# Attention and a maxout FFN on one core: batch 0 reordered, and loads issued behind the crossbar transpose's shift

## The chip, the cores and the metric

The kernel runs on one core of one Trainium2 chip. Time is device microseconds of that core, the median of repeated runs. The profile is one execution, recorded by the hardware profiler; instants in it are counted from its first instruction.

## The reference

Softmax attention with an extra exp(−m) in the denominator, then a feed-forward network whose hidden layer is the maximum of three products:

```python
scores = scale * np.matmul(q, k.transpose(0, 1, 3, 2))      # q, k, v: (8, 12, 448, 64)
m = np.max(scores, axis=-1, keepdims=True)
e = np.exp(scores - m)
attn = e / (np.sum(e, axis=-1, keepdims=True) + np.exp(-m) + 1e-09)
attn_out = np.matmul(attn, v)
x = attn_out.transpose(0, 2, 1, 3).reshape(B * S, H * D)    # 3584 x 768
h = np.maximum(np.maximum(x @ w1, x @ w2), x @ w3)          # 768 x 768 each
out = h @ w_out
```

Inputs and output are float32; the kernel computes in float16 with float32 sums.

## The kernel before

**Units of work.** The eight batches have twelve heads each. Four heads form a group, so a batch has three groups and there are 24 of them, numbered 0 to 23. For a group, `load_qk` (L91) and `load_v` (L108) bring q, k and v to SBUF and cast them to float16; POOL issues these loads. q and k must be transposed. Groups below `PE_QK` (6) are transposed by TensorE with an identity, `transpose_pe` (L172), and copied out of PSUM by DVE or ACT. Later groups go through the DMA crossbar, `transpose_dma` (L207): one DMA for QT and one for KT, issued by SP. QT then needs blocks copied to the other half of the partitions, `shift_q` (L216), four copies on POOL.

**Attention.** `scores` (L260) multiplies KT blocks with QT into PSUM tiles `stp` of the pool `ps_s` (three buffers), and ACT takes the exponential into `e`. `av_tail` (L304) and `av_main` (L323) multiply `e` with v, which `prep_v` (L354) has arranged in `vx` and `vt`; a column of constants beside v gives the sum of the exponentials. DVE adds the one, inverts and scales, into `xn`. `x_transpose_pe` (L367, TensorE and DVE) or `x_transpose_dma` (L382, a crossbar DMA from SP) puts `xn` into `xT`.

**FFN.** `up_piece` (L392) makes one slice of the hidden layer for one of the three weights: six matmuls for each 128 features in a tile `p_i` of the pool `ps_b` (two buffers), and DVE copies it or takes the maximum into `hT`. `out_piece` (L418) makes half of 128 output rows: six matmuls into `op_ps`, a scaling copy on DVE into `o_sb` (three buffers), and after the second half two stores of 64 rows from SP.

**Order.** The order on each engine is written out by hand. FFN pieces stand in a list; `fill` (L467) takes pieces from it while a credit in matmul columns lasts, so that FFN matmuls lie between attention matmuls.

- Batch 0 runs in six parts: its three groups with the even tokens ("E"), then with the odd ones ("O"). Part n computes scores of its group, then `av` of the part before, and at its end the x transpose of the part before. After the fourth part (n = 3), `add_up` puts nine FFN pieces for the even tokens in the list.
- From group 3 on, iteration i has three visits: scores of a third of group i in each, `av` of group i−1 in the first two, `prep_v(i)` and the x transpose of group i−1 in the second, and FFN pieces at the end of each. `adds` names the visits at which a further batch's FFN pieces enter the list; `share` spreads what is in the list over the visits until the next such visit.
- Iteration i begins with `transpose_dma(i + 2)` (SP), then the loads of v for group i+2 and of q and k for group i+3 (POOL), then the visits, and it ends with `shift_q(i + 2)` (POOL). QT and KT have three buffers, so the transpose of group i+2 waits for the scores of group i−1, and for the loads of group i+2. Each engine and each queue works in order: what stands behind a waiting instruction on SP or POOL waits too.

The lines that set this order in an iteration:

```python
        if i + 2 < NI and i + 2 >= PE_QK:
            transpose_dma(i + 2)
        ...
        elif i + 2 < NI:
            load_v(i + 2)
            if i + 3 < NI:
                load_qk(i + 3)
        for vi, units in enumerate(visits):
        ...
        if i + 2 < NI and i + 2 >= PE_QK:
            shift_q(i + 2, nc.gpsimd)
```

The functions in full:

Of the kernel before, what the change touches and what calls it, by code (L numbers as in the profile page):

```python
# [21 lines left out]
def kernel(  # L22
# [29 lines left out]
    scale = 1.0 / math.sqrt(D)  # L52


    PE_QK = 6
    NEB = 2
    NV = 3

# [32 lines left out]
    def load_qk(i, names="kq", prs=(0, NP)):  # L91
        b, g = groups[i]
        tiles = raw.setdefault(i, {})
        for nm in names:
            if nm not in tiles:
                t = ld_pool.tile([P, NP * T + 2, D], MMDT, tag="ld_" + nm, name="ld_" + nm)
                if nm == "q" and i < PE_QK:
                    nc.vector.memset(t[:, 0 : NP * T + 2 : NP * T + 1, :], 0.0)
                tiles[nm] = t
            src = {"q": q, "k": k}[nm][b].rearrange("h s d -> (h s) d")  # L100
            src = src.rearrange("(g r x t) d -> g x r (t d)", g=NG, r=NP, x=P)[g]
            p0, p1 = prs
            nc.gpsimd.dma_start(  # L103
                out=tiles[nm][:, 1 : NP * T + 1].rearrange("x (r t) d -> x r (t d)", r=NP)[:, p0:p1],
                in_=src[:, p0:p1],
            )
# [24 lines left out]
    nc.vector.memset(wz, 0.0)  # L131
    load_qk(0, "q")
    load_qk(0, "k", (0, 1))
    ident16 = cpool.tile([128, 128], MMDT, name="ident16")
    make_identity(nc, ident16)
    load_qk(0, "k", (1, 2))
    load_qk(1)
    load_v(0)
    load_qk(2)
# [32 lines left out]
    def transpose_pe(i, pr, pool, k_eng, q_engs):  # L172

        if pool is ps_s:
            both = ps_s.tile([128, 2, 1024], MMDT, tag="s", name="trT")
            tps = [both[:, 0], both[:, 1]]
        else:
            tps = [ps_b.tile([128, 1024], MMDT, tag="b", name="trT") for _ in range(2)]
        kr, qr = raw[i]["k"], raw[i]["q"]
        def tr(n, j, src, t):  # L180
            nc.tensor.transpose(  # L181
                out=tps[n][:, ts(j, 128)],
                in_=src[:, t + 1 : t + 3, :].rearrange("x t d -> x (t d)"),
                identity=ident16,
            )

        kj = (0, 1, 2) if pr == 0 else (3, 4, 5, 6)
        qt = (-1, 1, 3, 5, 0, 2, 4, 6) if pr == 0 else (8, 10, 12, 7, 9, 11, 13)
        for j, b in enumerate(kj):
            tr(0, j, kr, 2 * b)  # L190
        for j, t in enumerate(qt):
            tr(1, j, qr, t)
        if i not in KT:
            KT[i] = att_pool.tile([P, T * 128], MMDT, tag="KT", name="KT")
            QT[i] = att_pool.tile([P, (NB + 1) * 128], MMDT, tag="QT", name="QT")
        evac(
            k_eng,
            KT[i][:, kj[0] * 128 : (kj[-1] + 1) * 128],
            tps[0][:, 0 : len(kj) * 128],
        )  # L200
        q0 = pr * 1024
        n = -(-len(qt) // len(q_engs))
        for e, eng in enumerate(q_engs):
            a, b = e * n * 128, min((e + 1) * n, len(qt)) * 128
            evac(eng, QT[i][:, q0 + a : q0 + b], tps[1][:, a:b])
# [209 lines left out]
    NW = DM // NH  # L415
    order = (0, 2, 4, 6, 1, 3, 5)

    def out_piece(bp, t, nh):  # L418
        if nh == 0:
            outs[0] = out_pool.tile([128, DM], FP32, tag="o_sb", name="o_sb")  # L420
        o_sb = outs[0]
        op_ps = ps_b.tile([128, 512], FP32, tag="b", name="op_ps")
        for fc in range(NFC):
            nc.tensor.matmul(  # L424
                out=op_ps[:, 0:NW],
                lhsT=hT[bp][:, fc, ts(t, 128)],
                rhs=wout_sb[:, fc, ts(nh, NW)],
                start=(fc == 0),
                stop=(fc == NFC - 1),
            )  # L430
        nc.vector.tensor_scalar(  # L431
            out=o_sb[:, ts(nh, NW)],
            in0=op_ps[:, 0:NW],
            scalar1=1.0 / LAMBDA,
            scalar2=None,
            op0=ALU.mult,
        )
        if nh == NH - 1:
            for half in range(2):
                n = 2 * t + half  # L440
                b = 2 * bp + n // T
                rows = out[b * S : (b + 1) * S].rearrange("(p t) m -> t p m", t=T)
                nc.sync.dma_start(out=rows[order[n % T]], in_=o_sb[half * HP : half * HP + HP])


    UP = NDC * (S + 6)
# [3 lines left out]
    def add_up(b, q0, qn, order):  # L450
        w = 1 if qn == S else 2
        for i, f0 in order:
            fcs = tuple(range(f0, f0 + w))
            pieces.append((up_piece, (b, fcs, i, q0, qn), NDC * w * (qn + 6)))
# [12 lines left out]
    def fill(cols):  # L467
        credit[0] += cols
        while pieces and credit[0] > 0:
            f, a, w = pieces.pop(0)  # L470
            f(*a)
            credit[0] -= w
        if not pieces:
            credit[0] = min(credit[0], 0.0)
# [5 lines left out]
    DV, AC = nc.vector, nc.scalar  # L480
    warm(10)
    transpose_pe(0, 0, ps_s, DV, (AC, DV))
    transpose_pe(0, 1, ps_b, DV, (DV,))
    load_weight(0)
    prep_v(1, nc.gpsimd)
# [3 lines left out]

    parts = [(part, g) for part in "EO" for g in range(NG)]  # L490
    PW = {"E": (0, 1), "O": (2, 3), "EO": (0, 1, 2, 3)}
    UPE = 9 * 2 * NDC * (NE + 6) / 10

    def av(i, ej, pr, part):
        av_tail(i, ej, pr, PW[part])
        av_main(i, ej, pr, PW[part])

    for n, (part, g) in enumerate(parts):
        ej = n % NEB
        pp, pg = parts[n - 1] if n > 0 else (None, None)  # L500
        step = UPE if n > 3 else 0
        scores(g, ej, (0, 1), part)
        scores(g, ej, (2, 3), part)
        if n > 0:
            av(pg, 1 - ej, 0, pp)
        fill(step)
        if part == "E" and 0 < g < NG - 1:
            transpose_pe(g + 1, 0, ps_b, AC, (DV,))
        fill(step)
        scores(g, ej, (4, 5), part)  # L510
        scores(g, ej, (6,), part)
        if n > 0:
            av(pg, 1 - ej, 1, pp)
        if n == 0:
            transpose_pe(1, 0, ps_b, DV, (DV,))
        fill(step)
        if part == "E" and g < NG - 1:
            transpose_pe(g + 1, 1, ps_b, DV, (DV,))
        if n == 5:
            transpose_pe(3, 1, ps_s, DV, (DV,))  # L520
        fill(step)
        if n == 0:
            prep_v(0, DV)
        if n > 0:
            x_transpose_pe(pg, pp)
        if n == 1:
            load_weight(2)
        if n == 2:
            load_v(3)
            load_qk(4)  # L530
            load_weight(3)
        if n == 3:
            add_up(0, 0, NE, [(i, f) for i in range(3) for f in (0, 2, 4)])
        if n == 4:
            load_v(4)
            load_qk(5)
            transpose_pe(3, 0, ps_s, DV, (DV,))


    visits = ((0, 1), (2, 3), (4, 5, 6))  # L540
    adds = {3 * (3 * b + 4) + 1: b for b in range(1, B - 1)}

    def share(n):

        nxt = min([a for a in adds if a > n], default=3 * NI + 2)
        return left() / (nxt - n)

    for i in range(3, NI):
        ej, pj = (i + 1) % NEB, i % NEB
        first = i == 3  # L550
        if i + 2 < NI and i + 2 >= PE_QK:
            transpose_dma(i + 2)
        if first:
            load_v(5)
            load_qk(6)
        elif i + 2 < NI:
            load_v(i + 2)
            if i + 3 < NI:
                load_qk(i + 3)
        for vi, units in enumerate(visits):  # L560
            n = 3 * i + vi
            scores(i, ej, units)
            if vi < 2:
                av(i - 1, pj, vi, "O" if first else "EO")
            if vi == 1:
                prep_v(i, nc.vector if i < PE_QK else nc.gpsimd)
                if not first:
                    x_transpose_dma(i - 1)
            if n in adds:
                add_batch(adds[n])  # L570
            per = UPE if first and vi < 2 else share(n)
            if vi == 2 and first:
                fill(per / 2)
                x_transpose_pe(i - 1, "O")
                add_up(0, NE, NO, [(w, f) for w in range(3) for f in (0, 2, 4)])
                add_out(0)
                per = share(n)
            if vi > 0 and i + 1 < PE_QK:
                fill(per / 2)
                transpose_pe(i + 1, vi - 1, ps_s, DV, (DV,))  # L580
                fill(per / 2)
            else:
                fill(per)
        if i + 2 < NI and i + 2 >= PE_QK:
            shift_q(i + 2, nc.gpsimd)

    av(NI - 1, NI % NEB, 0, "EO")
    av(NI - 1, NI % NEB, 1, "EO")
# [34 lines left out]
```

## Time and profile before

| what | us |
|---|---|
| median of 13 runs (lowest, highest) | 348.16 (344.98, 356.18) |
| the profiled execution's own time | 347.0 |
| its span in the profile | 345.1 |
| TensorE (PE) busy | 329.1 |
| VectorE (DVE) busy | 191.7 |
| ScalarE (ACT) busy | 146.2 |
| GpSimd (POOL) busy | 139.4 |
| TensorE's last matmul ends | 340.0 |

The profiled execution's time is 1.9 us longer than its span, which runs from the first to the last instruction, and 1.2 us under the median of the runs. Busy times overlap, so they don't add up to the span. A busy PE means that a matmul is under way, not that the array is full; the mean clock granted to it was 0.994 of full speed. Instructions that only issue a DMA are not busy time on SP and ACT; on POOL they are.

### The profile page before, as it was taken

What the parts mean: (1) busy time and instruction counts of PE and PEld (TensorE: products, weight loads), DVE (VectorE), ACT (ScalarE), POOL (GpSimd) and SP (SyncE); (2) the same over time, 40 slices, a digit from 0 to 9 for tenths busy, and PEclk for the clock granted to TensorE, in tenths of its full rate; (3) what the DMA queues carried; (4) which work ended last, traced back from release to release, by engine and by line L of the source; (5) the groups of instructions that cost most, each with busy time, mean ns of one, the idle gap of its engine ahead of it and who ended that gap; (6) DMA issues with size and microseconds to landing.
All of it is one profiled execution on the core that took longest, in us unless ns stands there. A gap on an engine that the chain in (4) does not pass through costs nothing.

```text
span 345.1 us, 9731 instructions
## 1 busy us (share of the span) xinstructions
PE 329.1 (95%) x4150; PEld 198.8 (58%) x4150; DVE 191.7 (56%) x418; ACT 146.2 (42%) x174; POOL 139.4 (40%) x247
## 2 busy tenths in 40 slices
PE   7869989899999999999999999999999999999994
PEld 3547768765555555556555555556555555565552
DVE  2654576765555555555556556556556555565552
ACT  2863354676444435443443443444443443400000
POOL 8684540566094607633857065173535000000000
PEclk9998999999999999999999999999999999999999
DMA  7999999999999999999996999979951450124006
GB/s 95 192 207 209 205 201 143 146 118 198 145 180 148 164 141 220 155 94 157 226 171 106 178 180 136 146 87 233 166 95 21 123 123 3 31 62 108 2 16 167
DMA packets 89499, 47.42 MB, mean 137 GB/s; under 512 B 58224, under 2 KB 85872, under 8 KB 89456
## 3 DMA queue, kind: packets, MB, share of 16 engines
q0 software_dynamic: 29392, 22.03, 47.5%
q1 hardware_dynamic: 60064, 24.78, 43.6%
q8 instruction: 32, 0.52, 0.7%
q14 instruction: 11, 0.09, 0.1%
HBM read 44.04 MB, written 11.01 MB: 160 GB/s over the span
## 4 chain that ended last, share of the span: by engine, by line
PE 88%; DMA 4%; DVE 3%; issue 2%; ACT 2%; POOL 1%; ACTq 0%; POOLq 0%
PE p_i L401 46%; PE op_ps L424 16%; PE avp L331 11%; PE stp L274 11%; DMA ld_q<-in_q_dram 3%; PE avp L314 2%; ACT e L294 2%; PE trT L181 2%; DMA ld_k<-in_k_dram 1%; DVE xn L347 0%; DVE QT L170 0%; PE xtp L374 0%; POOL ld_k L103 0%; DVE hT L412 0%; DVE vt L360 0%
## 5 line engine op out<-in xcount | busy, mean ns | idle before, releaser
L294 ACT ACTIVATE e<-stp 128x896 f16<-128x896 f32 (+4 forms) x171 | 143.8, 903 | 147.8 <-PE stp L274 147.8
L401 PE MATMUL p_i<-xT,w 128*128 128x448 f16 (+2 forms) x972 | 174.4, 333 | 0.1
L401 PEld LDWEIGHTS <-w 128*128 128x128 f16 x972 | 90.4, 98 | 68.3 <-issue 5.0
L412 DVE TENSOR_TENSOR hT<-hT,p_i 128x448 f16<-128x448 f16 (+2 forms) x96 | 59.5, 621 | 42.3 <-PE p_i L401 42.0
L219 POOL COPY QT<-QT 64x384 f16<-64x384 f16 (+1 forms) x72 | 40.1, 556 | 104.1 <-DMA QT<-ld_q 73.9
L424 PE MATMUL op_ps<-w,hT 128*128 128x384 f16 x336 | 58.3, 326 | 0.4 <-DVE hT L412 0.4
L274 PE MATMUL stp<-QT,KT 64*64 64x448 f16 (+2 forms) x756 | 47.9, 339 | 3.9 <-ACT e L294 3.5
L331 PE MATMUL avp<-vx,e 128*128 128x65 f16 x1152 | 45.6, 194 | 0.0
L424 PEld LDWEIGHTS <-hT 128*128 128x128 f16 x336 | 31.6, 98 | 23.6 <-issue 2.6
L431 DVE TENSOR_SCALAR o_sb<-op_ps 128x384 f32<-128x384 f32 x56 | 31.1, 556 | 24.8 <-PE op_ps L424 24.8
L410 DVE CAST hT<-p_i 128x448 f16<-128x448 f32 (+2 forms) x48 | 30.0, 624 | 24.2 <-PE p_i L401 24.1
L331 PEld LDWEIGHTS <-e 128*128 128x128 f16 x1152 | 39.0, 98 | 2.3
L347 DVE TENSOR_TENSOR xn<-avp,rb 128x512 f16<-128x512 f32 (+1 forms) x54 | 34.1, 632 | 1.9
L341 DVE TENSOR_SCALAR rb<-avp 128x8 f32<-128x8 f32 (+1 forms) x54 | 8.9, 165 | 43.5 <-PE avp L331 43.5
L274 PEld LDWEIGHTS <-KT 64*64 64x64 f16 x756 | 15.8, 105 | 28.3 <-issue 25.1
L314 PEld LDWEIGHTS <-e 64*64 64x64 f16 x768 | 14.9, 108 | 8.3 <-issue 1.7
L103 POOL DMA_DIRECT2D ld_q<-in_q_dram x24 | 17.9, 744 | 4.2 <-DMA w<-in_moe_w_dram 1.2
L103 POOL DMA_DIRECT2D ld_k<-in_k_dram x25 | 17.9, 715 | 3.1 <-PE p_i L401 1.5
L357 POOL COPY vx<-ld_v 128x768 f16<-128x768 f16 x20 | 16.4, 818 | 5.5 <-issue 2.9
L314 PE MATMUL avp<-vt,e 64*64 64x65 f16 x768 | 15.7, 193 | 1.1 <-ACT e L294 0.8
L113 POOL DMA_DIRECT2D ld_v<-in_v_dram x24 | 15.1, 628 | 3.7 <-DMA ld_k<-in_k_dram 1.7
L116 POOL DMA_DIRECT2D ld_v<-in_v_dram x24 | 15.2, 635 | 1.9 <-DMA w<-in_moe_w_out_dram 1.2
(33 smaller groups left out, 84.8 us busy)
## 6 DMA issues: line engine op xcount, KB each, us to landing
out_dram<-o_sb SPq DMA_DIRECT2D x56, 192.0 KB, 3.1
ld_v<-in_v_dram POOLq DMA_DIRECT2D x48, 128.0 KB, 4.9
ld_q<-in_q_dram POOLq DMA_DIRECT2D x24, 224.0 KB, 7.9
ld_k<-in_k_dram POOLq DMA_DIRECT2D x23, 224.0 KB, 6.7
w<-in_moe_w_dram POOLq DMA_DIRECT2D x9, 384.0 KB, 9.8
w<-in_moe_w_out_dram POOLq DMA_DIRECT2D x3, 384.0 KB, 10.9
xT<-xn SPq DMA_TRANSPOSE x21, 4.9
QT<-ld_q SPq DMA_TRANSPOSE x18, 5.5
```

The lines of the kernel that those rows point to most:

```text
L103: nc.gpsimd.dma_start(out=tiles[nm][:, 1 : NP * T + 1].rearrange("x (r t) d -> x r (t d)", r=NP)[:, p0:p1], in_=src[:, p0:p1],)
L219: eng.tensor_copy(out=t[d0 : d0 + HP, o * 128 : (o + n) * 128], in_=t[s0 : s0 + HP, a * 128 : (a + n) * 128],)
L274: nc.tensor.matmul(out=stp[half * HP : half * HP + HP, par, j * qn : (j + 1) * qn], lhsT=k_block(i, pr, h2, x[half]), rhs=q_cols(i, pr, h2 ...
L294: nc.scalar.activation(out=dst, in_=src, func=AF.Exp, scale=scale)
L314: nc.tensor.matmul(out=ps[half * HP : half * HP + HP, hh, j * D1 : (j + 1) * D1], lhsT=eF[hh * HP : hh * HP + HP, o : o + HP], rhs=vt[hh * ...
L331: nc.tensor.matmul(out=ps[:, hh, j * D1 : (j + 1) * D1], lhsT=eF[:, o : o + 128], rhs=vx[:, 2 * pr + hh, (x[0]), 0:D1], start=False, stop= ...
L347: nc.vector.tensor_tensor(out=xn[i][:, pr, ws[0] : ws[0] + nw].rearrange("p j h d -> p h j d"), in0=acc[:, :, :, 0:D], in1=rb[:, :, 0:nw]. ...
L401: nc.tensor.matmul(out=p_i[:, j * qn : (j + 1) * qn], lhsT=w_sb[i][:, dc, ts(fc, 128)], rhs=xT[b][:, dc, q0 : q0 + qn], start=(dc == 0), s ...
L410: nc.vector.tensor_copy(out=dst, in_=src)
L412: nc.vector.tensor_tensor(out=dst, in0=dst, in1=src, op=ALU.max)
L424: nc.tensor.matmul(out=op_ps[:, 0:NW], lhsT=hT[bp][:, fc, ts(t, 128)], rhs=wout_sb[:, fc, ts(nh, NW)], start=(fc == 0), stop=(fc == NFC - 1),)
L431: nc.vector.tensor_scalar(out=o_sb[:, ts(nh, NW)], in0=op_ps[:, 0:NW], scalar1=1.0 / LAMBDA, scalar2=None, op0=ALU.mult,)
```

## The change

It has two parts.

The first reorders batch 0 and the ends. The x transpose of a part moves one part later. In the fourth part (n = 3, the first with odd tokens) a second x transpose, of the last group's even tokens, follows behind the scores, then `add_up`; the even tokens' FFN pieces are so in the list before that part's last two fills and not after them. Both `av` of that part stand ahead of its scores units (2, 3). `UPE`, the credit per fill, falls from a tenth to a twelfth of the nine pieces, as there are more fills. The identity is built behind both halves of the first k load. Three dummy matmuls are put ahead of group 0's second transpose and four ahead of group 1's first. Some PSUM copies move between DVE and ACT. `PE_QK` falls from 6 to 5, so group 5 goes through the crossbar; group 4's PE transposes move one visit earlier, with ACT copying. The very last output piece is copied in two halves by DVE and ACT, and its stores are split by columns and issued on SP's and ACT's queues. `adds` moves each batch's FFN pieces one visit later.

The second part is `loads()`: from iteration 5 on the loads of v for i+2 and of q and k for i+3 are issued at the end of the iteration, behind `shift_q(i + 2)` on POOL, not at its start. In iterations 3 and 4 they stay at the start.

```diff
-    PE_QK = 6
+    PE_QK = 5
...
     load_qk(0, "k", (0, 1))
+    load_qk(0, "k", (1, 2))
     ident16 = cpool.tile([128, 128], MMDT, name="ident16")
     make_identity(nc, ident16)
-    load_qk(0, "k", (1, 2))
...
+        if last and nh == NH - 1:
+            hw = NW // 2
+            c = nh * NW
+            nc.vector.tensor_scalar(
+                out=o_sb[:, c : c + hw], in0=op_ps[:, 0:hw], scalar1=1.0 / LAMBDA, scalar2=None,
+                op0=ALU.mult,
+            )
+            nc.scalar.activation(
+                out=o_sb[:, c + hw : c + NW], in_=op_ps[:, hw:NW], func=AF.Copy, scale=1.0 / LAMBDA
+            )
...
+        if last:
+            store(o_sb, bp, t, 0, ts(nh, NW), nc.sync)
+            store(o_sb, bp, t, 1, ts(nh, NW), nc.scalar)
...
     transpose_pe(0, 0, ps_s, DV, (AC, DV))
+    warm(3)
     transpose_pe(0, 1, ps_b, DV, (DV,))
...
-    UPE = 9 * 2 * NDC * (NE + 6) / 10
+    UPE = 9 * 2 * NDC * (NE + 6) / 12
...
-        step = UPE if n > 3 else 0
+        step = UPE if n > 2 else 0
+        nxt = g + 1 if part == "E" and g < NG - 1 else None
         scores(g, ej, (0, 1), part)
-        scores(g, ej, (2, 3), part)
+        if n != 3:
+            scores(g, ej, (2, 3), part)
         if n > 0:
             av(pg, 1 - ej, 0, pp)
+        if n > 1 and n != 4:
+            x_transpose_pe(parts[n - 2][1], parts[n - 2][0])
+        if n == 3:
+            av(pg, 1 - ej, 1, pp)
+            scores(g, ej, (2, 3), part)
         fill(step)
...
+        if n == 0:
+            warm(4)
+            transpose_pe(nxt, 0, ps_b, DV, (AC, DV))
+            prep_v(0, DV)
+        if n == 3:
+            x_transpose_pe(pg, pp)
+            add_up(0, 0, NE, [(i, f) for i in range(3) for f in (0, 2, 4)])
+        if nxt is not None:
+            transpose_pe(nxt, 1, ps_b, AC if n == 0 else DV, (AC, DV))
+        if n > 0 and n != 3:
             av(pg, 1 - ej, 1, pp)
...
-        if n > 0:
-            x_transpose_pe(pg, pp)
...
-    adds = {3 * (3 * b + 4) + 1: b for b in range(1, B - 1)}
+    adds = {3 * (3 * b + 4) + 2: b for b in range(1, B - 1)}
...
-        if first:
-            load_v(5)
-            load_qk(6)
-        elif i + 2 < NI:
-            load_v(i + 2)
+        def loads():
+            if i + 2 < NI:
+                load_v(i + 2)
             if i + 3 < NI:
                 load_qk(i + 3)
+
+        if i < 5:
+            loads()
...
+            if vi == 0 and first:
+                x_transpose_pe(1, "O")
...
-            if vi > 0 and i + 1 < PE_QK:
-                fill(per / 2)
-                transpose_pe(i + 1, vi - 1, ps_s, DV, (DV,))
-                fill(per / 2)
-            else:
-                fill(per)
+            if vi < 2 and i + 1 < PE_QK:
+                transpose_pe(i + 1, vi, ps_s, AC, (AC,))
+            fill(per)
         if i + 2 < NI and i + 2 >= PE_QK:
             shift_q(i + 2, nc.gpsimd)
+        if i >= 5:
+            loads()
```

More of the change, by code (lines that the diff above doesn't have):

```diff
@@ L416, with store @@
     order = (0, 2, 4, 6, 1, 3, 5)
+    def store(o_sb, bp, t, half, cols, eng):
+        n = 2 * t + half
+        b = 2 * bp + n // T
+        rows = out[b * S : (b + 1) * S].rearrange("(p t) m -> t p m", t=T)[order[n % T]]
+        eng.dma_start(out=rows[:, cols], in_=o_sb[half * HP : half * HP + HP, cols])
     def out_piece(bp, t, nh):
+        last = bp == B // 2 - 1 and t == 6
         if nh == 0:
@@ L430, in out_piece @@
             )
[L431 to L443, printed above, removed]
+        if last and nh == NH - 1:
[8 more added lines that the diff above has]
+            )
+        else:
+            nc.vector.tensor_scalar(
+                out=o_sb[:, ts(nh, NW)],
+                in0=op_ps[:, 0:NW],
+                scalar1=1.0 / LAMBDA,
+                scalar2=None,
+                op0=ALU.mult,
+            )
+        if last:
+            store(o_sb, bp, t, 0, ts(nh, NW), nc.sync)
+            store(o_sb, bp, t, 1, ts(nh, NW), nc.scalar)
+        elif nh == NH - 1:
+            store(o_sb, bp, t, 0, slice(0, DM), nc.sync)
+            store(o_sb, bp, t, 1, slice(0, DM), nc.sync)
     UP = NDC * (S + 6)
@@ L500 @@
         pp, pg = parts[n - 1] if n > 0 else (None, None)
-        step = UPE if n > 3 else 0
+        step = UPE if n > 2 else 0
+        nxt = g + 1 if part == "E" and g < NG - 1 else None
         scores(g, ej, (0, 1), part)
-        scores(g, ej, (2, 3), part)
+        if n != 3:
+            scores(g, ej, (2, 3), part)
         if n > 0:
             av(pg, 1 - ej, 0, pp)
+        if n > 1 and n != 4:
[3 more added lines that the diff above has]
+            scores(g, ej, (2, 3), part)
         fill(step)
-        if part == "E" and 0 < g < NG - 1:
-            transpose_pe(g + 1, 0, ps_b, AC, (DV,))
+        if nxt is not None and n > 0:
+            transpose_pe(nxt, 0, ps_b, AC, (DV,))
         fill(step)
@@ L511 @@
         scores(g, ej, (6,), part)
-        if n > 0:
+        if n == 0:
[8 more added lines that the diff above has]
+        if n > 0 and n != 3:
             av(pg, 1 - ej, 1, pp)
-        if n == 0:
-            transpose_pe(1, 0, ps_b, DV, (DV,))
         fill(step)
-        if part == "E" and g < NG - 1:
-            transpose_pe(g + 1, 1, ps_b, DV, (DV,))
         if n == 5:
@@ L521 @@
         fill(step)
-        if n == 0:
-            prep_v(0, DV)
-        if n > 0:
-            x_transpose_pe(pg, pp)
         if n == 1:
@@ L531 @@
             load_weight(3)
-        if n == 3:
-            add_up(0, 0, NE, [(i, f) for i in range(3) for f in (0, 2, 4)])
         if n == 4:
```

## The prediction

> **What bounds the kernel now.** I read the page's chain first: who holds the path.
>
> ```profile
> PE 88%; DMA 4%; DVE 3%; issue 2%; ACT 2%; POOL 1%; ACTq 0%; POOLq 0%
> ```
>
> TensorE holds 88% of the path. The page's slices show it at nine tenths or more from about 50 us to the end, so what it can still lose lies early and in the last microseconds. The waits of TensorE name the losses:
>
> ```profile
> PE stp L274 <- ACT e L294: 3.5, 7, 0.9
> PE xtp L374 <- DVE xn L347: 1.6, 2, 0.8
> PE warm L155 <- DVE wz L131: 1.2, 1, 1.2
> PE trT L181 <- DMA ld_k<-in_k_dram: 1.1, 1, 1.1
> ...
> PE xtp L374 <- DVE KT L170: 0.6, 1, 0.6
> ```
>
> Columns: who waited for whom, total us, times, longest. All waits together are some 11 us, all before 72 us. One more loss shows only as a clock, in the windows view (PE busy is the second number, the granted clock the one after the POOL column):
>
> ```profile
> 23.24:26.65 3.41, 2.04 (x57) 1.53 (x57) 1.69 (x7) 2.21 (x4) 1.87 (x4) 1.00 1.17 206
> 26.65:30.07 3.42, 3.42 (x48) 2.67 (x37) 1.03 (x4) 1.51 (x2) 0.80 (x3) 0.50 1.17 212
> ```
>
> After a stretch with TensorE busy for 2.04 of 3.41 us, the next 3.42 us ran at half clock.
>
> TensorE hides two other resources: the DMA engines, and POOL, which issues the loads. The DMA share (last but one) and GB/s (last) of three stretches: loads alone, crossbar transposes alone, both mixed:
>
> ```profile
> 108.00:110.00 2.00, 2.00 (x15) 0.92 (x16) 0.98 (x3) 0.00 (x0) 0.00 (x0) 1.00 1.53 191
> 114.00:116.00 2.00, 2.00 (x19) 1.09 (x12) 0.76 (x2) 1.96 (x3) 0.84 (x2) 1.00 1.30 276
> 123.00:130.00 7.00, 7.00 (x88) 3.82 (x77) 3.66 (x8) 3.69 (x5) 0.00 (x0) 1.00 1.60 107
> ```
>
> Mixed, 107 GB/s move where either kind alone moves 191 or 276. A QT transpose issued at 119.2 beside loads took 11.9 us to land, one issued alone at 255.97 took 3.0.
>
> **What the Trainium skill says.** "DMA: Bandwidth & Descriptors", section "Issuing engines are not separate DMA queues": DMAs issued from the scalar, sync or gpsimd engine end on the same 16 DMA engines and interleave. The trace agrees (11.9 against 3.0 us). "Advanced Engine Details and Errata", section "X-Bar Transpose (TRN2)": transposing DMAs are as fast as regular ones. True here alone (276 against 191 GB/s), not beside loads (107). "TensorE: Matmul & The Clock Gate", Part 1: the clock follows activity in windows of about 3.4 us; the two windows above agree.
>
> **The change, part by part**, against the profiled execution (span 345.1, time 347.0; the median of 13 runs is 348.16, so 1.2 above it). Negative is a gain.
>
> 1. X transposes one part later, even-token sums ahead of scores. The waits for xn and KT fall, 1.6 + 0.6 = −2.2. The instructions stay. What is late next is ACT's exp. With the first two sum pieces in the fourth part (1.3 us each) TensorE should stay busy in the window before 26.65; half of 3.42 us is −1.7 (bounds 0 and −1.7). ACT's other waits I leave.
> 2. Identity behind both key loads: the second half of k is issued at 2.66 instead of 3.20, when POOL has finished the first, so −0.5 at most; the identity, 0.6 us long, is still ready before the first load lands at 5.7. I take −0.3.
> 3. Dummies: 7 of 512 columns, 0.22 us each (448 columns take 0.19 in p_i), 1.5 us, three in the 1.1 us wait for k, four ahead of group 1's transposes, whose data landed at about 10.4. Part 2 shortens the first wait; I take +0.3 (−0.5 to +0.9; below nothing, because they may hold the clock).
> 4. Group 5 by crossbar: 22 PE transposes go, 0.69 + 0.61 = −1.3, and with their ps_s tile one exp wait of 0.89 at 61.6, of which I take half, −0.4. Two DMA transposes and four POOL copies come instead (part 6).
> 5. The last piece: DVE's 0.56 becomes two halves on DVE and ACT, about 0.3. The last two stores, issued one after the other (340.60 and 341.12), start together on SP's and ACT's queues: −0.3 − 0.5 = −0.8 (0 to −1.3).
>
> Sum of 1 to 5: −2.2 − 1.7 − 0.3 + 0.3 − 1.7 − 0.8 = **−6.4** (range −3 to −8).
>
> 6. **Loads behind shift_q**, from i = 5. This costs nothing only while slack covers it. Before, in iteration i POOL issued v of i+2 and q, k of i+3, then shift_q(i+2): loads of group j stood behind the shift of j−2. Now they stand behind the shift of j−1, and that shift waits for the transpose of j−1, which waits for the loads of j−1. Load, transpose, shift, next load become one serial chain, one turn per group, with no load beside a QT transpose. Its turn, from POOL's timeline and the DMA issues of windows:
>
> ```profile
> 227.65 0.62 POOL L113 DMA_DIRECT2D ld_v<-in_v_dram  x1
> ...
> 229.56 0.75 POOL L103 DMA_DIRECT2D ld_q<-in_q_dram  x1
> ...
> 238.12 2.38 POOL L219 COPY QT<-QT 64x384 f16<-64x384 f16 x4 [6.36 <-DMA QT<-ld_q]
> 240.44 0.62 POOL L113 DMA_DIRECT2D ld_v<-in_v_dram  x1
> ```
> ```profile
> ld_q<-in_q_dram POOLq DMA_DIRECT2D x1, 224.0 KB, 5.5
> ```
>
> First v to q issue 1.91; q to landing 5.5 in that block, 5.7 and 6.3 in the two others (173.6, 185.5) without a QT transpose beside them: 7.4 to 8.2, I take 7.4. QT's issue follows by 0.1. Issue to shift: 3.1 clean (255.97 to 259.08), 4.15 with stores ahead (233.97 to 238.12); I take 3.5, since stores still share the queue. Shift to next load 2.3. **A turn is 7.4 + 0.1 + 3.5 + 2.3 = 13.3 us**; from 12.4 (the shortest block, 6.9 at 240.44, and a clean QT) to 14.8 (8.2 and 4.15). TensorE's iterations take 12.85 (the 12-matmul visits, 100.84 to 267.95 over 13). So the chain is slower than the engine that it feeds, by 0.45 us a group.
>
> Where it starts: q of 5 lands at 49.9, its transpose runs beside loads of 6 until about 55.5 (group 6's, issued at 53.6 beside loads, took 5.8), the shift ends at 57.9, loads of 7 land at 65.3, their shift ends at 71.2. The shift of 22 then ends 15 turns later, at 71.2 + 15 × 13.3 = 270.7. Iteration 22 also needs prep_v(21) on POOL, 2.7 of issue and 1.4 of copies after that shift, against 0.6 after its own scores: 3.5 more, 274.2. TensorE alone would be there at 272.6 (its start in the trace) − 5.6 (parts 1 to 4) − 3.0 (adds moves each batch's FFN one visit later, a visit's share) = 264.0. **Stall: +10.2 us**, spread over iterations 7 to 22.
>
> On SP, transposes of xn and output stores stand behind the QT and KT transposes of i+2, so they come later too. The xT of a batch would land about 13 us after the shift of 3b+4, and adds asks for it 10 us into that iteration: 3 us of slack needed, the same as prep_v's. The fourth o_sb of an odd batch needs the first one's store; up to 4 us in an iteration, which feeds back as slack. I take nothing for it.
>
> Sum: −6.4 + 10.2 = +3.8, 347.0 + 3.8 = 350.8, say **351**; on the median's scale 352.
>
> **Rivals.**
> (a) Faster. Without mixing, loads land sooner, and a turn is under TensorE's 12.85. For it: in a quiet block the first v landed in 3.0 us, and the other 576 KB at 191 GB/s take 3.1, so q could land at 6.1; QT alone takes 3.1; the sum is 6.1 + 0.1 + 3.1 + 2.3 = 11.6. Then only iterations 7 to 9 stall, whose FFN share is small, about 3 us: 347.0 − 6.4 + 3 = 343.6; with no stall 340.6. Against it: the shortest block in the trace took 6.9. It decides at the turn where the stall equals 6.4, about 13.05 us.
> (b) No change: a turn of 12.95 to 13.15, gain and stall cancel, 345.5 to 348.5.
> (c) Much slower: a turn of 14.0, with stores beside the loads: 15 × 0.7 = 10.5 more, 361.
> (d) Early reordering gives nothing, because ACT's exps are late in its place; loses 3 of the gain: 354.
>
> **How the numbers follow.** What this kernel's measurement can tell from no change is about 0.5%, 1.7 us. Forecast with (c) and (d) 0.55; (b) 0.10; (a) 0.35. The likeliest case alone spans 349 to 358. The range takes in (a) at its stalled end and below, and (c) without the o_sb wait: 340.5 to 361.
>
> **What would show it.** Right: waits of TensorE for POOL QT or POOL vt from iteration 7 on, recurring, and POOL idle before shift_q put down to DMA QT in nearly every group; QT landing in 3 to 4 us instead of a median of 5.5; no half clock near 27 us; 22 fewer L181 transposes. Wrong: TensorE without waits after 90 us, the shift of 22 ending before 262; then the turn was under 12.7. If the early gaps before 45 us are still 8 us or more, part 1 was wrong.

## The result and the profile after

The changed kernel takes **378.94 us** (median of 11 runs, 374.31 to 381.56) against 350.09 for the kernel before (48 runs shared by all comparisons): ratio **1.086**, interval 1.081 to 1.090. The forecast was 351 us. Some executions of a kernel run a per cent or two longer at a lower clock, so ratios and intervals here leave those out, and as the execution profiled (383.5 us, span 381.8, mean clock 0.955) is one of them, its total is some 5 us above the median.

In this execution the span is 36.7 us longer than before. PE is busy 337.6 us against 329.1, so 8.5 us are matmuls that ran longer, and TensorE's idle time (span less busy) rose from 16.0 to 44.2 us, 28.2 more. The chain of the kernel after, by engine and by line:

```profile
PE 43%; DMA 35%; POOL 11%; ACT 4%; issue 3%; DVE 2%; SPq 1%; ACTq 0%; POOLq 0%; DVEq 0%
PE p_i L401 25%; DMA ld_q<-in_q_dram 21%; DMA QT<-ld_q 11%; PE op_ps L431 7%; POOL QT L219 6%; PE avp L331 4%; PE stp L274 4%; ACT e L294 2%; POOL ld_k L103 2%; POOL ld_v L116 2%; POOL ld_v L113 2%; DMA KT<-ld_k 1%; PE trT L181 1%; DMA ld_k<-in_k_dram 1%; SPq L211 1%
```

TensorE's share of the path fell from 88% to 43%. The second line spells out the loop of the forecast's part 6: `ld_q` 21%, `QT` 11%, the shift (POOL L219) 6% and POOL's issues of the next loads. But the waits of TensorE (total, times, longest, us) do not show the wait that the forecast named:

```profile
PE p_i L401 <- DVE o_sb L449: 23.8, 2, 14.4
PE p_i L401 <- DMA xT<-xn: 3.6, 1, 3.6
...
PE avp L314 <- POOL vt L359: 0.6, 1, 0.6
```

The loop is in the chain, yet TensorE stands for 23.8 us at DVE's copy into `o_sb`, in two waits. The longer one, on DVE and on SP's queue (start, duration, instruction; in brackets the idle time before it and its releaser):

```profile
130.08 0.55 DVE L449 TENSOR_SCALAR o_sb<-op_ps 128x384 f32<-128x384 f32 x1
146.37 1.02 DVE L449 TENSOR_SCALAR o_sb<-op_ps 128x384 f32<-128x384 f32 x2 [15.74 <-DMA out_dram<-o_sb]
```
```profile
126.25 1.22 SPq L211 DMA_TRANSPOSE QT<-ld_q  x1
127.56 1.25 SPq L211 DMA_TRANSPOSE KT<-ld_k  x1
128.90 1.26 SPq L384 DMA_TRANSPOSE xT<-xn  x1
139.78 1.22 SPq L211 DMA_TRANSPOSE QT<-ld_q  x1
141.09 1.25 SPq L211 DMA_TRANSPOSE KT<-ld_k  x1
142.43 2.46 SPq L422 DMA_DIRECT2D out_dram<-o_sb  x4
```

DVE needs an `o_sb` buffer and waits 15.7 us for a store to land. The store is issued at 142.43, because ahead of it in SP's order stands the QT transpose of the next group, which waits for its loads until 139.78. A transfer that nobody needs yet (QT of two groups on) holds one that TensorE is waiting for. After such a wait the clock is low (span and busy time of PE, then PEld, DVE, ACT, POOL; granted clock, DMA share, GB/s):

```profile
132.60:147.00 14.40, 0.03 (x5) 0.06 (x2) 0.63 (x2) 2.28 (x3) 7.13 (x13) 0.61 0.78 138
135.63:152.70 17.07, 5.72 (x16) 2.37 (x16) 2.27 (x4) 0.00 (x0) 6.43 (x12) 0.50 0.91 163
```

In the second stretch the granted clock is 0.50 until 6 us after the wait has ended. The eighteen `p_i` matmuls behind the wait take 6.37 us, most of it in this stretch; eighteen at full clock, from 158.42, take 3.57. So this is where PE's extra busy time comes from, in good part.

QT transfers, which no longer have loads beside them, do land sooner, as forecast. The DMA issues of the kernel after (KB each, median us to landing) have 3.1 for QT where the kernel before had 5.5, and 6.1 for `ld_q` where it had 7.9:

```profile
ld_q<-in_q_dram POOLq DMA_DIRECT2D x24, 224.0 KB, 6.1
xT<-xn SPq DMA_TRANSPOSE x21, 2.8
QT<-ld_q SPq DMA_TRANSPOSE x19, 3.1
```

### The profile page after: what moved, and what is told of

The parts are those of the page before. It is cut to its first block, busy times and chain, and to the rows that moved or that the text cites. A ratio compares the mean times of both kernels' runs of the same rounds, so it can differ in the third digit from the quotient of the medians.

```text
span 381.8 us, 9728 instructions
## 1 busy us (share of the span) xinstructions
PE 337.6 (88%) x4135; PEld 199.3 (52%) x4135; DVE 183.1 (48%) x405; ACT 151.0 (40%) x183; POOL 142.9 (37%) x254
## 4 chain that ended last, share of the span: by engine, by line
PE 43%; DMA 35%; POOL 11%; ACT 4%; issue 3%; DVE 2%; SPq 1%; ACTq 0%; POOLq 0%; DVEq 0%
PE p_i L401 25%; DMA ld_q<-in_q_dram 21%; DMA QT<-ld_q 11%; PE op_ps L431 7%; POOL QT L219 6%; PE avp L331 4%; PE stp L274 4%; ACT e L294 2%; POOL ld_k L103 2%; POOL ld_v L116 2%; POOL ld_v L113 2%; DMA KT<-ld_k 1%; PE trT L181 1%; DMA ld_k<-in_k_dram 1%; SPq L211 1%
## 5 line engine op out<-in xcount | busy, mean ns | idle before, releaser
L401 PE MATMUL p_i<-xT,w 128*128 128x448 f16 (+2 forms) x972 | 181.2, 342 | 30.2 <-DVE o_sb L449 23.8
L401 PEld LDWEIGHTS <-w 128*128 128x128 f16 x972 | 92.0, 100 | 105.6 <-issue 46.6
L219 POOL COPY QT<-QT 64x384 f16<-64x384 f16 (+1 forms) x76 | 42.3, 556 | 149.5 <-DMA QT<-ld_q 122.3
L314 PEld LDWEIGHTS <-e 64*64 64x64 f16 x768 | 14.6, 107 | 12.1 <-issue 2.6
L357 POOL COPY vx<-ld_v 128x768 f16<-128x768 f16 x21 | 17.2, 819 | 4.2 <-DMA ld_v<-in_v_dram 3.3
L113 POOL DMA_DIRECT2D ld_v<-in_v_dram x24 | 15.2, 635 | 2.0 <-DMA w<-in_moe_w_dram 1.5
```

Of the source, the lines that this page charges most:

```text
L219: eng.tensor_copy(out=t[d0 : d0 + HP, o * 128 : (o + n) * 128], in_=t[s0 : s0 + HP, a * 128 : (a + n) * 128],)
L314: nc.tensor.matmul(out=ps[half * HP : half * HP + HP, hh, j * D1 : (j + 1) * D1], lhsT=eF[hh * HP : hh * HP + HP, o : o + HP], rhs=vt[hh * ...
L401: nc.tensor.matmul(out=p_i[:, j * qn : (j + 1) * qn], lhsT=w_sb[i][:, dc, ts(fc, 128)], rhs=xT[b][:, dc, q0 : q0 + qn], start=(dc == 0), s ...
```

## Experiments

The open questions were three: which part costs the time; whether it is the `o_sb` wait or the serial loop; and what sets the loop's turn. Ratios are to the kernel before on the same chip. S(j) is the instant when the shift of group j ends.

**Which part costs.** One kernel keeps the reordering and issues the loads at the start; another keeps the kernel before and only moves the loads.

```diff
# e1_loads_at_start (from after)
-        if i < 5:
-            loads()
+        loads()
...
-        if i >= 5:
-            loads()
# e2_only_late_loads (from before): the loads from i = 5 on behind shift_q
```

> The changed kernel with the loads back at the start of every iteration; all else of the change stays. Theory (the loads behind the shift cause the whole loss; the reordering gains what was forecast): no wait of TensorE for DVE o_sb or xT, no half clock after 85 us, about 340.6 us, that is 6.4 us under the kernel before. Rival (moving the FFN a visit later and group 5 to the crossbar cost by themselves): still waits for o_sb of several us, 355 us or more.

> The kernel before with one edit: from iteration 5 on the loads are issued behind the shift. Theory (the late loads alone cause the loss): 367 to 378 us, with waits of TensorE for xT, o_sb or POOL. Rival (it takes the later adds and group 5's transpose by DMA too, which start the chain one group earlier): under 358 us.

e1 took 347.17 us, ratio 0.997 (0.988 to 1.006); e2 369.63, 1.065 (1.059 to 1.071). So the late loads alone cost 6.5% of the 8.6%; the reordering alone is not told from no change, though e1 was expected 6.4 us faster. Waits of e1:

```profile
PE p_i L401 <- DMA xT<-xn: 1.9, 1, 1.9
PE trT L181 <- DMA ld_k<-in_k_dram: 1.5, 1, 1.5
PE avp L314 <- POOL vt L359: 1.2, 1, 1.2
...
PE avp L314 <- DVE xn L347: 1.2, 2, 0.9
PE trT L181 <- ACT KT L168: 1.0, 1, 1.0
PE stp L274 <- ACT QT L168: 0.9, 1, 0.9
```

The old waits of `stp` for ACT's exp (3.5 us) and of `xtp` for `xn` and KT are gone, and waits of the same size have come at other places: copies that ACT now makes (KT, QT), `xn` again, and two late ones for `vt` and `xT`. The other 2% come only when the reordering is added to the late loads (1.065 to 1.086): e2 waits 9.4 us for `o_sb`, the kernel after 23.8. Moving `adds` back by one visit, alone, tests why:

```diff
# e5_adds_back (from after)
-    adds = {3 * (3 * b + 4) + 2: b for b in range(1, B - 1)}
+    adds = {3 * (3 * b + 4) + 1: b for b in range(1, B - 1)}
```

> The changed kernel with adds one visit earlier again, as before the change; loads stay behind the shift. It puts four stores of an odd batch ahead of the next group's transposes on SP. Theory (it is the combination of later adds and later loads that parks the first store behind a transpose of the next iteration): o_sb waits shrink from 23.8 us to some 10, waits for xT grow from 3.6 us to about 8, total 360 to 370 us. Rival (the visit makes no difference, the loads alone park the stores): 376 to 382 us with two waits of 9 to 14 us.

It took 373.68, ratio 1.073 (1.063 to 1.083), with 9.9 us of `o_sb` and 10.7 of `xT` waits: the waits were as expected, the time above the expected interval. The later `adds` puts the first stores of an odd batch behind one more QT transpose; but with 14 us less of that wait and 7 more for `xT` it is only about 5 us faster.

**The `o_sb` wait or the loop.** Three kernels take the wait away: by buffers, by another queue, and by SP's order.

```diff
# e3_osb6 (from after)
-    out_pool = ctx.enter_context(tc.tile_pool(name="outp", bufs=3))
+    out_pool = ctx.enter_context(tc.tile_pool(name="outp", bufs=6))
# e4_stores_act (from after)
-            store(o_sb, bp, t, 0, slice(0, DM), nc.sync)
-            store(o_sb, bp, t, 1, slice(0, DM), nc.sync)
+            store(o_sb, bp, t, 0, slice(0, DM), nc.scalar)
+            store(o_sb, bp, t, 1, slice(0, DM), nc.scalar)
# h1_transpose_behind_stores (from after), for i >= 5
-        transpose_dma(i + 2)      # at the start of the iteration
+        if vi == 2: transpose_dma(i + 2)   # ahead of the third visit's scores
```

> The changed kernel with six output buffers instead of three. Theory (the two long waits are for stores that stand behind a crossbar transpose on SP): both o_sb waits of 14.4 and 9.4 us go, and with them the half clock that follows (some 5 us), but the serial chain load, transpose, shift stays and binds next: new waits for POOL QT or vt at about 0.5 to 1 us an iteration, the shift of group 22 ends at 279 to 290 us, total 358 to 370 us. Rival A (the chain isn't binding at all): 352 us, no waits after 100 us. Rival B (stores are slow because of contention, not of order): the waits stay, 375 us or more.

> The changed kernel with all output stores issued from ACT's queue instead of SP's, three buffers. Theory (order on SP is what delays the stores): o_sb waits gone as with six buffers, 358 to 370 us, within 5 us of that kernel; ACT loses some 0.6 us for each store's issue, which its idle time takes. Rival (buffers are too few whatever the queue, since stores land late): the waits of 9 to 14 us stay, 375 us or more.

> The changed kernel with its three output buffers and its late loads, v first; from iteration 5 on transpose_dma(i + 2) is recorded at the third visit, so that on SP it stands behind the stores and the xn transpose of iteration i and not ahead of them. The loads, which the transpose waits for anyway, stay where they were. Theory (the o_sb waits are stores parked behind a transpose that waits for late loads): these waits fall from 23.8 us to under 6, waits for POOL vt come instead, as with six buffers, and the time is 362 to 372 us. Rival (three buffers are short on their own): o_sb waits of 9 us or more stay, 374 us or more.

e3: 372.10, ratio 1.071 (1.061 to 1.082), 2 us above the expected interval. h1: 378.05, 1.090 (1.077 to 1.104). e4: 375.82, 1.077 (1.065 to 1.088). e3's waits of TensorE, then h1's:

```profile
PE avp L314 <- POOL vt L359: 15.6, 7, 3.9
PE p_i L401 <- DMA xT<-xn: 3.0, 1, 3.0
```
```profile
PE avp L314 <- POOL vt L359: 16.1, 7, 4.4
...
PE p_i L401 <- DVE o_sb L449: 0.6, 2, 0.4
```

Both remove nearly all of the 23.8 us of `o_sb` wait, and both show in its place the wait that the forecast had named: TensorE for `vt`, seven times, since `prep_v` stands on POOL behind the shift. h1 is the cleaner proof of where the `o_sb` wait came from, since it changes only what stands ahead of the stores on SP; it saves nothing, where 362 to 372 us were expected, and e3 saves some 5 us. Why h1 is slower than e3 at the same `vt` waits was not settled; its TensorE is busy 340.3 us against 336.9. The long wait for `o_sb` had hidden a loop that is just as late: S(22) is 294.1 us in the kernel after and 294.2 in h1. In e4 the stores sit on ACT's queue, where one waits 8 us and ACT's exps stand behind it, so it says nothing about the loop; its expectation failed for that reason. ACT in e4 (the profile puts the idle time down to a QT transfer, but the stores ahead of the exp were out only at 98.27):

```profile
90.29 7.98 ACTq L422 DMA_DIRECT2D out_dram<-o_sb  x2
98.37 4.16 ACT L294 ACTIVATE e<-stp 128x896 f16<-128x896 f32 x5 [10.72 <-DMA QT<-ld_q]
```

**What sets the turn.** POOL in e3, shifts and first loads of three groups, and the DMA issues of the second of these blocks:

```profile
125.50 2.38 POOL L219 COPY QT<-QT 64x384 f16<-64x384 f16 x4 [6.46 <-DMA QT<-ld_q]
127.83 0.63 POOL L113 DMA_DIRECT2D ld_v<-in_v_dram  x1
...
140.90 0.63 POOL L113 DMA_DIRECT2D ld_v<-in_v_dram  x1
...
142.83 0.74 POOL L103 DMA_DIRECT2D ld_q<-in_q_dram  x1
...
158.04 0.62 POOL L113 DMA_DIRECT2D ld_v<-in_v_dram  x1
```
```profile
out_dram<-o_sb SPq DMA_DIRECT2D x3, 192.0 KB, 5.1
...
ld_q<-in_q_dram POOLq DMA_DIRECT2D x1, 224.0 KB, 9.6
xT<-xn SPq DMA_TRANSPOSE x1, 7.7
```

From first `ld_v` to first `ld_v` it is 13.1 us, then 17.1. In the first of the two turns nothing was issued beside the loads and `ld_q` landed after 5.6 us; in the second, stores and an xT transpose were issued beside them and it took 9.6. That is 4.0 us, the whole difference. The other turns agree: of the 15 from S(7) to S(22) in e3, the five with four or more stores issued between the shift and the next QT took 15.4 to 17.4 us, nine of the others 12.7 to 13.6 and one 15.1. Four of the five had an xT transpose too; the one with stores alone took 15.4. To test it, a kernel that is e3 but leaves out the stores of the first six batches:

```diff
# g4_few_stores (from e3)
-        elif nh == NH - 1:
+        elif nh == NH - 1 and bp == B // 2 - 1:
```

> The changed kernel with six output buffers that stores only the last quarter of the output (the first three pairs of batches aren't written out). Theory (every third turn of the chain is 16 to 17 us instead of 13 because output stores and the xn transpose flow beside the loads): those turns shrink to 13 to 14 us, the average turn from 14.5 to about 13.3, the vt waits from 15.6 to 2 to 8 us, the time from 372 to 350 to 360 us. Rival (the long turns come from the loads alone or from waits on SP): the turns stay at 16 to 17 us, 368 us or more.

It took 363.82, ratio 1.048 (1.043 to 1.054), above the 350 to 360 expected. The turn from S(7) to S(22) averages 13.65 against 14.5 in e3, none is above 15.2, and the `vt` waits fall from 15.6 to 4.2 us. The stores are worth 0.85 us a turn, most of what the average had above 13.3. One wait of 3.5 us for `xT` stays. Now the other way: leave the stores, and shorten the loop by issuing what it waits for first.

```diff
# f1_osb6_q_first (from e3); g1_q_first is the same with bufs=3 (from after)
         def loads():
+            if i + 3 < NI:
+                load_qk(i + 3, "qk" if i >= 5 else "kq")
             if i + 2 < NI:
                 load_v(i + 2)
-            if i + 3 < NI:
-                load_qk(i + 3)
```

> The changed kernel with six output buffers, and in each late block the loads of q and k issued ahead of v (q first) instead of behind it. Theory (with the buffers no longer short, the serial chain load, transpose, shift sets the pace, 14.5 us a turn against 12.85 us of TensorE work): q is issued 1.9 us sooner in its block and lands at least 1.2 us sooner after the shift, so the turn falls to about 13 us, the waits of TensorE for POOL vt fall from 15.6 to under 4 us, and the time from 372 to 350 to 356 us. Rival (the vt waits come from POOL being late with prep_v for another reason, or from DMA bandwidth): the waits stay above 10 us and the time above 365 us.

> The changed kernel with three output buffers as it has, and in each late block the loads of q and k ahead of v. It separates the parked stores from the long turn. Theory (the store waits exist because the transposes ahead of them on SP wait for late loads; a turn of 12 us brings those transposes forward): o_sb waits fall from 23.8 us to under 3, 345 to 349 us. Rival (three buffers are short on their own once adds is a visit later): o_sb waits of 9 us or more stay, 355 us or more.

f1: 345.61, ratio 0.996 (0.994 to 0.999), better than the 350 to 356 expected and what e1 takes without late loads. g1: 356.11, 1.027 (1.023 to 1.031). One turn in f1, on POOL and in the DMA issues:

```profile
109.04 0.71 POOL L103 DMA_DIRECT2D ld_q<-in_q_dram  x1
...
118.46 2.38 POOL L219 COPY QT<-QT 64x384 f16<-64x384 f16 x4 [5.30 <-DMA QT<-ld_q]
120.79 0.71 POOL L103 DMA_DIRECT2D ld_q<-in_q_dram  x1
```
```profile
ld_q<-in_q_dram POOLq DMA_DIRECT2D x1, 224.0 KB, 3.7
...
QT<-ld_q SPq DMA_TRANSPOSE x1, 5.5
```

3.7 for q, 5.5 for QT, 2.4 for the shift: 11.75 us a turn, under TensorE's 12.85. From S(7) to S(22), where the first iterations are shorter, the average is 12.0, as in the kernel before (71.1 to 250.9): the loop keeps up with TensorE. QT is slower here than in e3, since it now runs beside k and v; the loop is shorter all the same, because the 1.9 us of v and k issue and their share of the transfer are out of it. g1 was expected at 345 to 349 and missed: one `o_sb` wait of 8.6 us stays. Here too the stores (issued at 127.91) stand behind a QT transpose that waited for its loads (124.58). Three buffers are not short by themselves: e1 has three and the later `adds`, and no `o_sb` wait. The four kernels side by side, us and ratio:

| | v first, then q and k | q first |
|---|---|---|
| three `o_sb` buffers | 378.94, 1.086 (after) | 356.11, 1.027 (g1) |
| six | 372.10, 1.071 (e3) | 345.61, 0.996 (f1) |

By the ratios, which compare kernels on the same chip, the order of the issues is worth 5.9 or 7.5% (20 or 26 us) and the buffers 1.5 or 3.1% (5 or 11 us). The loop is the main cause and the parked stores a second one.

**What is left of the reordering.** Loads at the start again, group 5 back on TensorE (f3), and then `adds` back too (f4); g2 and g3 put q first, g3 with late loads and six buffers.

```diff
# f3_qk6 (from e1); f4_qk6_adds1 also has adds at +1
-    PE_QK = 5
+    PE_QK = 6
# g2_f4_q_first: f4 with loads() as in f1; g3_late_q_first_qk6_adds1: f1 with PE_QK = 6 and adds at +1
```

> The changed kernel with the loads at the start of every iteration and group 5 transposed by TensorE again (PE_QK 6); the later adds stay. Theory (the gain of the reordering is eaten by waits for xT and vt near 80 to 88 us, which group 5's crossbar transpose causes by sharing the DMA engines early): those waits fall from 3.8 us to under 1.5, the 22 transposes cost 1.3 us; about 1 us faster than with PE_QK 5. Rival (the waits come from the early pace, not from the transpose): no faster than with PE_QK 5, 347 to 349 us.

> As the one with loads at the start and PE_QK 6, and adds back at the earlier visit: of the change only the reordering of batch 0 and the last piece are left. If these two gain what was forecast for them (waits for xn, half clock, tail, less dummies: some 4 us), 344 us where the kernel before has 348 to 351. If the early waits only move from xn to ACT's and DVE's copies, 346 to 348 us.

> Loads at the start, PE_QK 6, adds at the earlier visit, and q and k loaded ahead of v from iteration 5 on. TensorE has no waits after 70 us in the same kernel with v first, so an earlier q has nothing to shorten: within 1 us of its 344.4. Rival (fewer slow executions, as the load slack grows): median 343 us.

> Late loads with q and k ahead of v, six output buffers, PE_QK 6 and adds at the earlier visit. Theory: with a turn of 12 us the late loads cost nothing, and nothing is gained by them either, since TensorE doesn't wait for the DMA engines in the kernel with loads at the start: 344 to 345 us, the same as that. Rival (the late loads gain something once the chain is short): under 343 us. Rival (xT, asked for a visit earlier, is late): waits for xT of 2 to 5 us, 347 us or more.

f3: 345.97, ratio 1.000 (0.997 to 1.002), not told from e1 (0.997), where 1 us faster was expected. f4: 344.35, 0.994 (0.991 to 0.996). g2: 344.30, 0.993 (0.990 to 0.995). g3: 344.11, 0.993 (0.991 to 0.995). So the batch 0 reordering with its last piece gains 0.6%, some 2.2 us; the later `adds` take about 1.6 of it back (f3 against f4; why was not shown); and late loads, once the loop is short, neither gain nor cost. f4, g2 and g3 beat both kernels, and are not told apart.

## Why the prediction was wrong

The direction and the mechanism of part 6 were right: a serial loop of load, transpose, shift and next load, slower than TensorE. 351 was too low by 28 us, and 361, the end of the range, by 18. Step by step:

- **The turn, 13.3 us, was mis-sized, in its first term.** The forecast gave q 5.5 us from issue to landing in every turn and put the stores into QT's 3.5 alone. In the quiet turns of e3 this held: QT, which waits for q, was issued 5.3 to 6.2 us after it, and the turns took 12.7 to 13.6; QT landed in 3.0 (median of all). In the five turns with stores beside the loads QT came 8.0 to 9.8 us after q, and the turns took 15.4 to 17.4. The average is 14.5 in e3 (S(7) = 72.5, S(22) = 290.0) and 14.6 in the kernel after (75.2 to 294.1). S(22), forecast at 270.7, so came 23.4 us late: 19.4 by the turns and 4.0 by a later S(7), forecast at 71.2. The three blocks from which 5.5, 5.7 and 6.3 were read had at most two stores issued before q landed, and so said little about turns with four to six. Rival (c) had this mechanism; its 14.0 was still too small.
- **The rest of the sum held.** With the measured S(22) and the forecast's 3.5 us for `prep_v`, e3's iteration 22 should have its `av` at 293.5; the trace has it at 293.77, after a wait for `vt`. That is 19.6 us behind the forecast's 274.2 and makes 370.4 us; the execution profiled took 371.7. The early gain drops out there, since TensorE waits for the loop. In the kernel after the same working gives 297.6, and the `av` comes at 305.95: the other 8.3 us are not the loop's but the `o_sb` waits', since TensorE waits for nothing more after the second of them, which ended at 236.41. That makes 350.8 + 23.4 + 8.3 = 382.5 us; the execution profiled took 383.5.
- **"I take nothing for it", on `o_sb`, failed.** The forecast let the fourth `o_sb` wait up to 4 us, for a store behind one transpose that is already under way. The trace shows the stores behind the *next* QT transpose, which waits for loads that stand behind a shift: 14.4 and 9.4 us. By the table it is worth 5 us with the long loop. Waits that overlap don't add: taking one away exposes the other.
- **A term was missing: the half clock after a stall.** The forecast used the clock window as a gain at 27 us, and priced its own stalls without it. Busy time is 337.6, 336.9 and 340.3 us in the kernel after, e3 and h1, which stall, and 328.5, 328.9 and 329.5 in e1, f4 and f1, which don't: 7 to 12 us, which lie within the delays above. Of the busy time, 15.9 us in the kernel after and 10.1 in e3 lie in stretches at half clock, and none in e1. Matmuls take about twice as long there (6.37 against 3.57 us for eighteen), so about half of that, 7.9 and 5.1 us, is an estimate of the cost; what is left over was not explained. The Trainium skill, "TensorE: Matmul & The Clock Gate", Part 1, says that the clock follows activity in windows of about 3.4 us. The traces agree on the window: three waits in e3, of 2.0, 3.4 and 3.9 us, were each followed by 3.41 us at half clock. Two others, of 3.0 us each, were not, so the length of a wait alone does not decide. The stretch after the shortest of them, which ended at 105.16:

```profile
105.37:108.78 3.41, 3.28 (x44) 2.32 (x43) 1.06 (x3) 0.00 (x0) 0.09 (x1) 0.50 0.80 120
```

- **The gain of parts 1 to 5, −6.4, was too large.** Measured: −1.0 in e1 (−4 to +2 by its interval), −2.2 in f4. The half clock at 27 us did go, as forecast; the kernel after has:

```profile
23.24:26.65 3.41, 2.68 (x56) 1.93 (x54) 2.19 (x8) 1.90 (x4) 1.24 (x2) 1.00 1.17 210
26.65:30.07 3.42, 3.42 (x60) 2.94 (x59) 1.67 (x4) 1.01 (x2) 1.41 (x2) 1.00 1.17 213
```

  After TensorE had been busy for 2.68 of 3.41 us (before: 2.04) the clock stayed at 1.00. What failed is "the waits for xn and KT fall", −2.2: waits of the same kind came at other pieces. TensorE's gaps before 45 us did fall, from 8.2 us to between 5.9 and 7.4 in the kernels with the reordering, so the sign that the forecast named for part 1 (8 us or more) did not show; but the seven dummies stand in these gaps, 1.5 us by the forecast's own price, and do no work. The end, −0.8, was −0.4: from the last matmul to the last landing it is 3.79 us before, 3.39 after. Group 5 by crossbar, −1.7: the 22 transposes went (132 to 110), and f3 against e1 shows no gain from it. Rival (d), "loses 3", had the size about right, but not its reason: the waits of `stp` for ACT's exp fell from 3.5 us to 0.2.
- **Rival (a)** was right that transfers land sooner unmixed and wrong that this brings the turn under 13.05. f1 shows the reverse: with QT beside loads again and a shorter loop the turn was 12.0. The forecast's own case of mixing, a QT of 11.9 us, was not loads alone: four output stores were issued at 122.66, before it landed. In f1 QT took 5.1 us (median).
- **The signs named.** Recurring waits for `vt` were right, but visible only where `o_sb` didn't stall first (e3, h1). The Trainium skill's "DMA: Bandwidth & Descriptors", section "Issuing engines are not separate DMA queues", says that DMAs of all issuing engines interleave on the same 16 engines. It bears on every part here: the second turn in e3 was lengthened by SP's stores beside POOL's loads (9.6 against 5.6 us). The forecast cited it for QT, and left stores beside the loads to rival (c).

## What to carry to other kernels

Before moving a load behind something on an in-order queue, write down the loop of dependences that this closes, and price its turn with everything that shares the DMA engines in any turn, stores too; an average turn decides, and a chosen quiet block gives its lower bound. Then walk each queue for what is parked behind a waiting instruction (here stores behind a transpose), and when a wait is removed, ask which loop is just behind it. To speed up such a loop, issue first what it waits for: here the order of the loads was worth 20 to 26 us, while issuing them late gained nothing even where the loop was short (g3 against f4).

## What was not expected of the hardware

A transposing DMA beside casting loads is slower (QT 5.1 us median in f1 against 3.1 without), as was expected, but here that cost nothing: f1 takes 345.61 with it, e3 372.10 without. And a stall of TensorE need not be long to be paid twice: a wait of 2.0 us was followed by 3.4 us at half clock, though two of 3.0 us were not.
